# A Fourier layer with a routed expert layer on one core: order of ScalarE's relu, GpSimd's sums and expert pieces in each step

## The chip, the cores and the metric

The kernel runs on one core of a Trainium2 chip. The metric is the device time of one execution in microseconds (us); the runs shown take 745.76, 746.71 and 750.62 us, median 746.71. The engines are called as in the profile: PE is TensorE's matmuls, PEld its weight loads, DVE is VectorE, ACT is ScalarE, POOL is GpSimd, and SP is SyncE, which here only issues DMA transfers.

## The reference, cut to what matters

```python
def _attn_ref(x, w_r, w_i, b_r, b_i):            # x: 8 x 3136 x 256, fp32
    X = np.fft.rfft(x, axis=1)
    Yr = Xr @ w_r - Xi @ w_i + b_r
    Yi = Xr @ w_i + Xi @ w_r + b_i
    Yr = np.sign(Yr) * np.maximum(np.abs(Yr) - lam, 0.0)      # lam = 0.01, Yi alike
    return np.fft.irfft(Yr + 1j * Yi, n=3136, axis=1)

def _moe_ref(x, w_gate, w1, w2, capacity):        # x: what _attn_ref returned; capacity 128
    scores = np.einsum('bsd,d->bs', x, w_gate)
    out = x.copy()
    for b in range(B):
        top_idx = the `capacity` rows of b with the highest scores
        ye = np.maximum(x[b, top_idx] @ w1, 0.0) @ w2
        out[b, top_idx] = x[b, top_idx] + sigmoid(scores[b, top_idx])[:, None] * ye
    return out
```

## The kernel before

Each of the 8 batches goes through a forward transform in two stages, a product with the complex weights, a soft threshold, and an inverse transform in two stages. Between the stages of a transform the data lie in scratch memory in HBM, As on the way forward and Cs on the way back.

- First forward stage: `fold` (lines 420 to 431) makes a sum and a difference of two halves of an input tile xt, two POOL additions at L425 into a tile sd; `s1` (L444) multiplies sd on PE, ACT copies the result to at (L447), and SP stores it to As.
- Second forward stage and the spectrum, in units of one group g of a batch b: `ld_a` loads av from As (four groups at once), and for the last group of two batches together a small tile at, two loads of 64 KB. `s2` (L492, for the last group L500) makes px; ACT casts it to Xh (L504) and DVE takes the rest Xl (L505).
- `spectral` (lines 507 to 526): six matmuls into the second half of the PSUM bank pcb, which ACT copies to ks (L519) and POOL adds to the bias as kb (L521); twelve matmuls into py (L237 to L239 are the lines of the helper that issues all eighteen); DVE adds kb to py (L525).
- `shrink` (lines 528 to 533): ACT's relu r of py (L530) and DVE's Y (L532), which together are the soft threshold.
- First inverse stage, `s2i` (from line 535): eight matmuls from Y (L553) into the first halves of the banks pca and pcb. Then, in this order, ACT copies pca into ct (L565), DVE takes the scores from pcb (L567, a product with the gate's weights that is summed into Csc; the name "junk" is its unused product), ACT copies pcb, and DVE takes the scores from pca. SP stores ct to Cs, where the last stage fetches it as cv.
- Last inverse stage, `s1i` (from line 617), 32 calls in all: 32 matmuls (L626), two ACT copies (L635 into ot, L642 into a tile of the pool sd), and four additions and subtractions on POOL (L639), which `finish` puts into the list adds; the last entry of a call puts the 1 MB store of ot to the output into the list waiting, from where `flush` hands it to SP at the start of a later step. There are two ot buffers, so that a call needs the store of the call before last to be over.
- The expert layer: once a batch's scores are there, `select` finds the 128th score digit by digit with short matmuls into pca (L264) and short DVE instructions (L250 to L286), `place` the rows, `gather` fetches them (xe, L352), and `ffn` multiplies them in pieces: transposes at L363, pairs of matmuls at L388 and single ones at L404. One call of `tick(ffns)` issues one piece.

The order on every engine is written by hand; each engine works its instructions off in that order. The main loop runs over t, one step a unit, with T = 100. A step issues, in this order: the SP stores and loads of the step; s2 of unit t + 1; an s1 if one is due, else one expert piece; the routing's matmuls; spectral of unit t; the fold that is due (L848 to L851; `steady` names the folds that are due); `add(n)`, the next n entries of adds (L852); s1i where the step has one; `ticks` expert pieces (L837); s2i of unit t - 1; shrink of unit t (L869); and finish. After the loop a tail does the routing of the last batch, the rest of s1i and three experts.

## Time and profile before

| | before |
|---|---|
| runs (us) | 745.76, 746.71, 750.62; median 746.71 |
| profiled execution (us) | 751.31 |
| its span, first to last instruction (us) | 749.5 |
| PE busy, share of the span | 666.2 us, 89% |
| PEld | 491.0 us, 66% |
| DVE | 444.6 us, 59% |
| ACT | 377.9 us, 50% |
| POOL | 445.5 us, 59% |
| mean granted clock of PE | 0.96 of 2.4 GHz |

The engines run side by side, so busy times don't add up to the span. A matmul's end is modelled in the profile, and matmuls overlap: a busy PE may still have started its next matmul late, which is seen from the starts alone. The idle time before an instruction and what ended it are in square brackets in a timeline, and in the list of waits as a sum over the program.

### The profile page before, as it was taken

The page shows a single profiled execution, that of the slowest core. Times are in us where ns is not written, and L with a number is a line of the kernel's source. Part 1 is how long each engine was busy: PE and PEld are TensorE (multiplying, and loading weights), DVE is VectorE, ACT ScalarE, POOL GpSimd, SP SyncE. Part 2 cuts the span into 40 slices and gives each one's busy share as a digit, 9 for nine tenths or more (in the row PEclk, how much of TensorE's full clock was granted, in tenths as well). Part 3 has the DMA queues.
Part 4 walks back from the last instruction along what each step waited for, and adds up shares of the span by engine and source line. Part 5 has one row for each costly group of instructions (what it writes and reads, how often), then busy time and mean ns, then how long its engine had stood idle before and what let it go on. Part 6 is the DMA issues. An engine that isn't in the chain of part 4 may idle for free.

```text
span 749.5 us, 21755 instructions
## 1 busy us (share of the span) xinstructions
PE 666.2 (89%) x8923; PEld 491.0 (66%) x8923; DVE 444.6 (59%) x1386; ACT 377.9 (50%) x672; POOL 445.5 (59%) x369
## 2 busy tenths in 40 slices
PE   6599899999898888998999889998998889978896
PEld 2476667766666666776776577665776677656475
DVE  5255556875777465765767455775567566665450
ACT  4155545556556565555555465564555454544310
POOL 1266555367777577666667567675745466475471
PEclk9899999999999899999999899999999999999877
DMA  9979758778788697778587786978484865745650
GB/s 315 324 280 329 240 172 269 242 244 312 224 302 283 241 320 242 257 255 284 162 281 248 254 284 192 329 237 280 147 255 146 271 194 187 232 141 172 211 208 21
DMA packets 96642, 179.62 MB, mean 240 GB/s; under 512 B 5758, under 2 KB 83424, under 8 KB 85216
## 3 DMA queue, kind: packets, MB, share of 16 engines
q1 hardware_dynamic: 95360, 175.96, 69.6%
q0 software_dynamic: 896, 2.17, 0.9%
q8 instruction: 70, 1.15, 0.6%
q14 instruction: 28, 0.23, 0.1%
q10 hardware_dynamic: 288, 0.11, 0.1%
HBM read 92.31 MB, written 85.98 MB: 238 GB/s over the span
## 4 chain that ended last, share of the span: by engine, by line
PE 42%; DVE 14%; POOL 12%; DMA 11%; ACT 10%; issue 9%; SPq 1%; POOLq 0%; DVEq 0%; ACTq 0%
PE pca L553 7%; POOL kb L521 6%; DMA at<-As 4%; PE py L237 4%; DVE junk L567 4%; PE s L444 3%; ACT r L530 3%; PE px L626 3%; POOL sd L425 3%; PE py L238 3%; PE py L239 3%; DVE Xl L505 3%; PE m L388 2%; PE px L492 2%; POOL ot L639 2%
## 5 line engine op out<-in xcount | busy, mean ns | idle before, releaser
L521 POOL TENSOR_TENSOR kb<-ks,bias 128x512 f32<-128x512 f32 x100 | 128.0, 1280 | 228.2 <-ACT ks L519 209.1
L639 POOL TENSOR_TENSOR ot<-ot,sd 128x512 f32<-128x512 f32 x120 | 153.8, 1283 | 4.7
L425 POOL TENSOR_TENSOR sd<-xt 113x512 f32<-113x512 f32 x104 | 130.5, 1279 | 20.0 <-DMA xt<-in_x 20.0
L505 DVE TENSOR_TENSOR Xl<-px,Xh 128x768 fp32r<-128x768 f32 x100 | 95.8, 958 | 44.5 <-ACT Xh L504 44.5
L525 DVE TENSOR_TENSOR py<-py,kb 128x512 f32<-128x512 f32 x100 | 69.8, 698 | 80.1 <-POOL kb L521 62.0
L553 PE MATMUL pca<-Y,gi_sb 64*64 64x256 f32 x760 | 103.2, 390 | 7.6 <-DVE pca L259 4.5
L553 PE MATMUL pcb<-Y,gi_sb 64*64 64x256 f32 x768 | 104.8, 390 | 0.0
L532 DVE SCALAR_TENSOR_TENSOR Y<-py,r 128x512 f32<-128x512 f32 x100 | 69.2, 692 | 45.5 <-ACT r L530 45.4
L565 ACT COPY ct<-pca 128x256 f32<-128x256 f32 x99 | 37.0, 373 | 108.9 <-PE pcb L553 100.3
L492 PEld LDWEIGHTS px<-g_sb,av 64*64 64x64 f32 x3072 | 76.9, 135 | 22.6 <-ACT ot L635 8.0
L504 ACT CAST Xh<-px 128x768 fp32r<-128x768 f32 x100 | 80.9, 809 | 18.1 <-PE px L492 12.8
L492 PE MATMUL px<-g_sb,av 64*64 64x96 f32 x3072 | 83.5, 246 | 5.0 <-DVE Xl L505 2.0
L553 PEld LDWEIGHTS pca<-Y,gi_sb 64*64 64x64 f32 x760 | 46.5, 133 | 56.6 <-DVE pca L259 15.2
L567 DVE CUSTOM_DVE_ANT_0 junk<-pcb,wgb 128x256 f32<-128x256 f32 x100 | 42.3, 423 | 61.0 <-PE pcb L553 54.8
L447 ACT COPY at<-s 128x1024 f32<-128x1024 f32 x58 | 59.6, 1027 | 33.4 <-PE s L444 33.4
L530 ACT ACTIVATE r<-py,m2l 128x512 f32<-128x512 f32 x100 | 69.4, 694 | 5.7 <-DVE py L525 5.7
L237 PE MATMUL py<-wnh,Xh 128*128 128x256 f32 x200 | 63.8, 319 | 7.2 <-DVE Y L532 5.7
L444 PE MATMUL s<-sd,w 64*64 64x512 f32 x480 | 67.8, 623 | 2.4 <-ACT at L447 2.2
L237 PE MATMUL pcb<-wsh,Xh 128*128 128x256 f32 x200 | 66.7, 333 | 3.2 <-ACT ct L565 3.2
L635 ACT COPY ot<-px 128x1024 f32<-128x1024 f32 x30 | 30.4, 1012 | 67.7 <-PE s L626 59.9
L239 PE MATMUL py<-wnl,Xh 128*128 128x256 f32 x200 | 57.3, 286 | 0.0
L238 PE MATMUL py<-wnh,Xl 128*128 128x256 f32 x200 | 57.2, 286 | 0.0
(183 smaller groups left out, 1482.7 us busy)
## 6 DMA issues: line engine op xcount, KB each, us to landing
out<-ot SPq DMA_DIRECT2D x30, 1024.0 KB
xt<-in_x SPq DMA_DIRECT2D x28, 1024.0 KB
av<-As SPq DMA_DIRECT2D x46, 512.0 KB
Cs<-ct SPq DMA_DIRECT2D x23, 1024.0 KB
cv<-Cs SPq DMA_DIRECT2D x90, 256.0 KB
As<-at SPq DMA_DIRECT2D x28, 784.0 KB
cv<-in_x SPq DMA_DIRECT2D x4, 1024.0 KB
out<-at SPq DMA_DIRECT2D x2, 1024.0 KB
```

Of the source, the lines that this page charges most:

```text
L237: nc.tensor.matmul(out, wh, mh, start=start, stop=False)
L238: nc.tensor.matmul(out, wl, mh, start=False, stop=False)
L239: return nc.tensor.matmul(out, wh, ml, start=False, stop=stop).ins
L425: eng.tensor_tensor(out=f[:113, k], in0=t[:113, 0], in1=t[:113, 1], op=op)
L444: nc.tensor.matmul(p[64 * c:64 * c + 64, r, :], w[64 * r:64 + NH * r, v, :], f[64 * r:64 + NH * r], start=(k == 0), stop=(k == len(parts[0 ...
L492: nc.tensor.matmul(o[:, :, N2 * j:N2 * j + N2], a[64 * p:64 * p + 64, j, g % 4, 128 * h + 64 * q:128 * h + 64 * q + 64], g_sb[64 * p:64 * ...
L504: nc.scalar.copy(out=vh, in_=v)
L505: nc.vector.tensor_tensor(out=vl, in0=v, in1=vh.bitcast(F32), op=ALU.subtract)
L521: nc.gpsimd.tensor_tensor(out=kb[:r], in0=ks[:r].broadcast_to([r, 2, D]), in1=bias[:r], op=ALU.add)
L530: nc.scalar.activation(out=r1[:r], in_=py[:r], func=AF.Relu, bias=m2l[:r], scale=1.0)
L553: nc.tensor.matmul(p[q][64 * a:64 * a + 64], gi_sb[64 * q:64 * q + 64, g, c, 64 * a:64 * a + 64], y[64 * q:64 * q + 64, c, :], start=(c == ...
L639: return lambda: nc.gpsimd.tensor_tensor(out=o[:, k, r], in0=o[:, 0, r], in1=q[:, r], op=(ALU.add, ALU.subtract)[k])
```

## The change

There are three edits, all to the order of instructions; none adds or removes arithmetic.

1. The relu of unit t moves on ACT from behind the two copies of s2i(t - 1) to between them. `s2i` takes a function `between`, which it calls after the first copy and the first score; `shrink` takes the finished relu. It holds for steps 1 to T - 2.
2. The four sums of an s1i call: a step that issues a fold (or has one due in the plan, `steady(t + LEAD + 2)`) now takes one entry of adds, another step two; before, a step took two entries of five and then three. The hand-over of the store is no longer an entry of its own but belongs to the last sum.
3. A step issues one or two expert pieces in place of two or three.

```diff
-    def shrink(b, g, py, r):
+    def relu(py, r):
         r1 = pool.tile([128, 2, D], F32, name="r1", bufs=RB)
         nc.scalar.activation(out=r1[:r], in_=py[:r], func=AF.Relu, bias=m2l[:r], scale=1.0)
+        return r1
+
+    def shrink(b, g, py, r, r1=None):
+        r1 = r1 or relu(py, r)
         y = pool.tile([128, 2, D], F32, name="Y", bufs=YB)
         nc.vector.scalar_tensor_tensor(out=y[:r], in0=py[:r], scalar=0.0, in1=r1[:r], op0=ALU.min, op1=ALU.add)
         Y[b, g] = y
 
-    def s2i(b, g):
+    def s2i(b, g, between=None):
...
             nc.vector.tensor_tensor_reduce(out=junk, in0=p[k], in1=wgb, scale=1.0, scalar=0.0,
                                            op0=ALU.mult, op1=ALU.add, accum_out=Csc[bk][:, col:col + 1])
+            if k and between:
+                r1 = between()
...
+        return r1 if between else None
...
         def finish():
             nc.scalar.copy(out=q, in_=p[1])
-            adds.extend([op(0, 1), op(0, 0), op(1, 1), op(1, 0), lambda: waiting.append((done["t"] + 3, store))])
+            last = op(1, 0)
+            adds.extend([op(0, 1), op(0, 0), op(1, 1), lambda: (last(), waiting.append((done["t"] + 3, store)))])
             if b == B - 1:
-                add(5)
+                add(4)
...
-        ticks = 2 + (t % 3 > 0) if t < T - 1 else 0
+        ticks = 1 + (t % 3 > 0) if t < T - 1 else 0
...
-        add(3 if len(adds) < 5 else 2)
+        add(1 if steady(t + LEAD + 2) and len(adds) < 5 else 2)
...
-            s2i(b, g)
+            r1 = s2i(b, g, (lambda: relu(py, r)) if t < T - 1 else None)
...
-            shrink(*units[t], py, r)
+            shrink(*units[t], py, r, r1 if t > 0 else None)
```

ACT, two neighbouring steps in the middle of the loop (ct is the copy of s2i, r with a number is the relu, sd the second copy of s1i). Before:

```order
L565 COPY ct<-pca 128x256
L565 COPY ct<-pcb 128x256
L530 ACTIVATE r_5592<-py,m2l 128x512
L642 COPY sd<-s 128x1024
L504 CAST Xh<-px 128x2x6x64
L519 COPY ks<-pcb 128x256
```

and with the change (its line numbers differ by a few):

```order
L569 COPY ct<-pca 128x256
L530 ACTIVATE r_5577<-py,m2l 128x512
L569 COPY ct<-pcb 128x256
L649 COPY sd<-s 128x1024
L504 CAST Xh<-px 128x2x6x64
L519 COPY ks<-pcb 128x256
```

The relu and the second copy have changed places; what follows them is the same.

POOL, about a period of s1i near step 40 (kb belongs to spectral, sd<-xt is the fold, ot<-ot,sd are the sums). Before:

```order
L521 TENSOR_TENSOR kb<-ks,bias 128x512
L425 TENSOR_TENSOR sd<-xt 113x512 x2
L639 TENSOR_TENSOR ot<-ot,sd 128x512 x2
L521 TENSOR_TENSOR kb<-ks,bias 128x512
L425 TENSOR_TENSOR sd<-xt 113x512 x2
L521 TENSOR_TENSOR kb<-ks,bias 128x512
L639 TENSOR_TENSOR ot<-ot,sd 128x512 x2
L521 TENSOR_TENSOR kb<-ks,bias 128x512
```

and with the change:

```order
L521 TENSOR_TENSOR kb<-ks,bias 128x512
L425 TENSOR_TENSOR sd<-xt 113x512 x2
L646 TENSOR_TENSOR ot<-ot,sd 128x512
L521 TENSOR_TENSOR kb<-ks,bias 128x512
L425 TENSOR_TENSOR sd<-xt 113x512 x2
L646 TENSOR_TENSOR ot<-ot,sd 128x512
L521 TENSOR_TENSOR kb<-ks,bias 128x512
L646 TENSOR_TENSOR ot<-ot,sd 128x512 x2
L521 TENSOR_TENSOR kb<-ks,bias 128x512
```

Between two kb there were up to four POOL instructions, with the change there are at most three, and the four sums of a call end one step later.

SP, the loads of the small tile at for step 60 (at_ with a number) and what stands around them (Cs<-ct stores, out<-ot stores, av and xt loads). Before:

```order
L164 DMA Cs_74<-ct 1024x1x256
L164 DMA out<-ot 128x2048
L164 DMA at_5599<-As 64x1x256 x2
L164 DMA av<-As 128x4x256 x2
L164 DMA As<-at 98x2048
L164 DMA xt<-in_x 128x2048
```

and with the change:

```order
L164 DMA Cs_74<-ct 1024x1x256
L164 DMA at_5586<-As 64x1x256 x2
L164 DMA av<-As 128x4x256 x2
L164 DMA As<-at 98x2048
L164 DMA out<-ot 128x2048
L164 DMA xt<-in_x 128x2048
```

The output store stands a step later, behind the small loads; 19 output stores move in such a way, and at the same place of step 35 it is likewise, while ahead of the loads for step 85 the store stays where it was.

## Rows read from the trace of the kernel before

**Rows 1.** Page, part 1: busy us (share of span) and instructions of PE.

```profile
PE 666.2 (89%) x8923; PEld 491.0 (66%) x8923; DVE 444.6 (59%) x1386; ACT 377.9 (50%) x672; POOL 445.5 (59%) x369
```

**Rows 2.** Waits, whole program: who <- for whom: us in total, times, longest.

```profile
DVE Y L532 <- ACT r L530: 45.4, 99, 0.8
...
ACT ct L565 <- DVE Csc L567: 32.1, 95, 1.3
...
PE py L237 <- DVE Y L532: 5.7, 18, 0.4
...
PE pcb L237 <- ACT ct L565: 3.2, 8, 0.6
```

**Rows 3.** Timeline of PE, step 12: start us, us, engine, instruction; last pcb, first py matmul.

```profile
104.99 0.28 PE L239 MATMUL pcb<-wsl,Xh 128*128 128x256 f32 x1
105.11 0.28 PE L237 MATMUL py<-wnh,Xh 128*128 128x256 f32 x1
```

**Rows 4.** The same two matmuls, steps 2 and 98.

```profile
49.04 0.28 PE L239 MATMUL pcb<-wsl,Xh 128*128 128x256 f32 x1
49.76 0.35 PE L237 MATMUL py<-wnh,Xh 128*128 128x256 f32 x1 [0.44 <-DVE Y L532]
...
675.26 0.28 PE L239 MATMUL pcb<-wsl,Xh 128*128 128x256 f32 x1
675.58 0.36 PE L237 MATMUL py<-wnh,Xh 128*128 128x256 f32 x1
```

**Rows 5.** Timeline of ACT, DVE, PE, step 84 into 85; [idle before <-releaser].

```profile
581.93 0.38 ACT L565 COPY ct<-pca 128x256 f32<-128x256 f32 x1 [2.57 <-PE pcb L553]
582.09 0.42 DVE L567 CUSTOM_DVE_ANT_0 junk<-pcb,wgb 128x256 f32<-128x256 f32 x1 [0.19 <-PE pcb L553]
...
582.56 0.37 ACT L565 COPY ct<-pcb 128x256 f32<-128x256 f32 x1 [0.25 <-DVE Csc L567]
...
582.83 0.69 ACT L530 ACTIVATE r<-py,m2l 128x512 f32<-128x512 f32 x1
...
583.55 0.69 DVE L532 SCALAR_TENSOR_TENSOR Y<-py,r 128x512 f32<-128x512 f32 x1 [0.45 <-ACT r L530]
...
584.07 0.28 PE L239 MATMUL pcb<-wsl,Xh 128*128 128x256 f32 x1
...
584.39 0.35 PE L237 MATMUL py<-wnh,Xh 128*128 128x256 f32 x1
```

**Rows 6.** Waits of ACT's relu, and POOL's groups by line (busy us, mean ns, idle before).

```profile
ACT r L530 <- DVE py L525: 5.7, 2, 3.4
...
L639 POOL TENSOR_TENSOR ot<-ot,sd 128x512 f32<-128x512 f32 x120 | 153.8, 1283 | 4.7
```

**Rows 7.** Timeline of SP and PE around the small loads for step 60.

```profile
404.48 0.61 SPq L164 DMA_DIRECT2D out<-ot  x1
405.15 2.28 SPq L164 DMA_DIRECT2D at<-As  x2
...
413.59 0.38 PE L553 MATMUL pcb<-Y,gi_sb 64*64 64x256 f32 x2
414.37 0.54 PE L500 MATMUL px<-gt_sb,at 64*64 64x192 f32 x4 [0.40 <-DMA at<-As]
416.27 1.22 PE L500 MATMUL px<-gt_sb,at 64*64 64x192 f32 x10 [1.36 <-DMA at<-As]
```

**Rows 8.** Stretches: PE, PEld, DVE, ACT, POOL busy (x), PEclk, DMA share, GB/s.

```profile
200.00:300.00 100.00, 89.92 (x1296) 65.41 (x1293) 62.52 (x195) 55.72 (x99) 68.53 (x55) 0.97 0.82 275
```

**Rows 9.** Chain that ended last: start us, us, two runs of expert matmuls.

```profile
310.86 0.89 PE m L388 x8
...
317.98 1.06 PE m L404 x4
```

**Rows 10.** Timelines of SP and ACT: an output store, and the reuse of its buffer.

```profile
493.89 1.10 SPq L164 DMA_DIRECT2D out<-ot  x1
...
509.82 1.01 ACT L635 COPY ot<-px 128x1024 f32<-128x1024 f32 x1 [3.17 <-PE s L626]
```

## The prediction

> **What bounds the kernel now.** The page comes first: PE is busy for 89% of the span [rows 1], all others for 50 to 66%, so a gain has to come out of PE's path. The list of waits comes second. PE's own entries are small: it is put down as waiting 5.7 us for Y and 3.2 us for the copies [rows 2]. But the profile models a matmul's end, and a matmul that starts late behind a modelled end leaves no idle time. So I read PE's starts in the timeline, third. Each step has six matmuls into pcb and then twelve into py. Where nothing holds them, the first py matmul starts 0.12 us after the last pcb matmul [rows 3]. In step 2 it starts 0.72 us after, in step 98 0.32 us after [rows 4], in step 85 0.32 us after, which is 0.15 us after Y ended at 584.24 [rows 5]. Py may not be overwritten before Y has read it, so Y holds PE. From step 2 to 98 I count 69 of 97 starts held like this (step 2 is the first, step 98 the last), together 17.2 us over the free spacing.
>
> Why is Y late? Y waits 45.4 us for the relu, in 99 steps [rows 2]. The relu stands behind both copies on ACT, and the second copy waits for DVE's score from the same bank: 32.1 us in 95 steps, 0.34 us each [rows 2]. In one of them [rows 5] the first copy ends at 582.31, the pcb score at 582.51, the second copy runs from 582.56 to 582.93, the relu from 582.83 to 583.52, and Y starts at 583.55 after DVE stood idle for 0.45 us.
>
> **Edit 1, the relu between the copies.** ACT starts a second instruction 0.10 us before the first one ends (582.83 against 582.93 [rows 5]). Put right behind the first copy, the relu runs from 582.21 to 582.90. DVE is free from 583.55 - 0.45 = 583.10, so Y starts at 583.13 in place of 583.55: 0.42 us earlier, more than the 0.20 us by which py was held in this step (0.32 less 0.12). The second copy then starts at 582.80 in place of 582.56, 0.24 us later; the score of pcb is long over. Behind that copy PE's next pcb matmul is queued, and behind that all of PE. In nine steps, nearly the eight that the list has as waits for the copy [rows 2], that matmul starts 0.05 us after it, so nine times 0.24 = 2.2 us are lost; elsewhere PE is busy with px and s1 or with the routing first. SP's Cs store waits for the copy too, 0.24 us, which a transfer of several us hides. ACT's last of the three ends at 583.17 in place of 583.52, so the cast Xh, Xl and DVE's selection chain behind it come 0.35 us earlier. The relu now needs kb's addition to py earlier, and would hold the second copy if that were late; it has waited for it only twice, 5.7 us [rows 6].
>
> The Trainium skill (PSUM — Partial Sum Buffer, section "PSUM bank collisions raise a hardware error") says that two engines may not touch one bank on the same partitions at once, reads included, while different banks are free. The trace agrees for the copy, which starts 0.05 us after the score ends [rows 5]; by that rule the relu, which reads py's bank, need not wait for it. If ACT had to wait for any DVE read of PSUM, the relu would start at 582.56, Y would gain 0.27 in place of 0.42 us, and the sum would end some 8 us higher.
>
> Bounds of edit 1: where PE binds every step, 17.2 - 2.2 = 15 us; where ACT's and DVE's chain binds every step, the idle time that the relu fills, 32.1 us. Both kinds of step stand in the trace, so I take the middle, 24 us.
>
> **Edit 2, the sums.** One sum takes 1.28 us [rows 6]; all 120 remain. A step with a fold had kb, two fold instructions and two sums, five times 1.28 = 6.4 us, against a mean step of (675.26 - 49.04) / 96 = 6.5 us [rows 4]: POOL came late to the next kb as soon as a step was shorter. With one sum the step has 5.1 us. What that gave to the path is bounded by the relu's waits for py, 5.7 us [rows 6], and by nothing, since most late kb are covered by PE's own work. I take 2 us.
>
> What moves with the sums is the store. The last sum of a call falls a step later, so 19 of the 1 MB output stores are issued a step later and change places on SP's queue. Twice (steps 35 and 60) a store leaves the place right ahead of the small loads at, for which PE waits. In step 60 [rows 7] the store is issued at 404.48, the loads at 405.15, PE is through with s2i at about 413.97 (413.59 + 0.38), waits 0.40 us and then 1.36 us for the loads and goes on at 416.27. 1 MB at the 275 GB/s of a full stretch [rows 8] is 3.8 us. Without it ahead, the last load lands at about 412.5, before PE asks. That is 1.76 us at each of two places, 3.5 us; a third such place, in step 85, keeps its store ahead. Ends: 0 us if the loads' lateness has another cause, 7 us if the slow restart behind the wait goes too. I take 4 us.
>
> The Trainium skill (DMA: Bandwidth & Descriptors, section "Queues, rings and completion order") says that a DMA engine takes a ring's descriptors in order. By that the store's transfer time comes off the landing, 4 us in the sum; if a small load could overtake, it would be 0. The trace leans to the rule: 128 KB took 11.1 us from issue to the last matmul's release [rows 7].
>
> **Edit 3, the expert pieces.** They are moved, not removed. Eight L388 matmuls, four pieces, take 0.89 us [rows 9], so a step loses about 0.22 us of pieces where an expert runs and gains it where none ran. Four matmuls of the fifth expert slide behind the loop into the tail, at most 1.06 us [rows 9], where filler matmuls stood. Thinner pieces may fill PE's waits for the routing. I take 0, with ends of -1 and +2 us.
>
> **Sum.** 24 + 2 + 4 + 0 = 30 us. The profiled execution took 751.3 us, 4.6 us over the median of the runs; 751.3 - 30 = 721.3, and on the scale of the runs 717 us. The low ends give 15 + 0 + 0 - 1 = 14 us, 733; the high ends 32 + 6 + 7 + 2 = 47 us, 700. The forecast's own range is 700 to 733.
>
> **Rivals.**
> - The transfers become the bound. The DMA share is already 0.82 between 200 and 300 us [rows 8]; steps that are 4% shorter ask for 0.86, and av, xt or cv may come late. Then half of edit 1 is lost, 12 us: 717 + 12 = 729 us. For it: PE waited for at [rows 7]. Against: the other loads are issued two or more steps ahead, and at is the only one with a wait of weight.
> - PE is really busy, and the late starts are how the profile draws pipelined matmuls. Then only the listed waits go, 5.7 us for Y less 2.2 us for the copy, about 743 us, no change that shows. For it: 89% busy [rows 1]. Against: the same two matmuls lie 0.12 us apart when Y is early [rows 3] and 0.72 us when it is late [rows 4].
> - Slower: the output store, a step later, is not over when its buffer is wanted. For the tightest of them: issue at 493.89, ACT writes the buffer again at 509.82, 15.9 us [rows 10]. A step less leaves 9.4 us. A store that needed as long as at did, 11.1 us [rows 7], would hold ACT's ot copy, all of ACT behind it and PE's px for 1.7 us. It decides against the kernel once the mean hold over 19 stores passes (30 + 7.5) / 19 = 2.0 us; at 3 us each the time is 717 + 57 = 774 us. Against: the store stands ahead of at in the queue and so ends sooner than 11.1 us, and the other stores have more room.
> - The change doesn't do what it says: excluded by the order of the instructions.
>
> **Chances.** A measurement of this kernel tells about 1% from no change, so faster is under 739.2 us and slower over 754.2 us. The forecast has 0.72, a still larger gain (under 700 us) 0.03, the transfers 0.10: faster 0.85. The busy PE has 0.09, all of it within 1%. The late stores have 0.06, slower. The range of 700 to 738 us takes in the forecast and the transfers' case, 0.82.
>
> **What would show it.** Right: the wait of the second copy for DVE's score falls from 32.1 us to nearly 0, Y's wait for the relu falls from 45.4 us to below 10, py starts 0.12 us after pcb in nearly all steps, and PE's waits for at shrink to the place in step 85. Wrong: PE's waits for the second copy rise well over 3.2 us (edit 1 gives its gain back at pcb); ACT's ot copy waits for a DMA (late stores); the relu's wait for py grows over 6 us (kb late, with the copy and PE held behind it); PE waits for av or cv (transfers); or the tail is longer by more than 1 us.

## The result, and the profile after

The changed kernel takes 719.69 us, the median of three runs (714.92 to 721.53), where the kernel before takes 746.71: a ratio of 0.9612, with a 95% interval of 0.9522 to 0.9703. Timed again beside its own variants it took 715.35 us against 746.47 (ratio 0.957, 0.9525 to 0.9616). The forecast was 717 us. The profiled execution of after took 714.92 us, its span is 713.2 us.

The page, part 1 (busy us, share of the span, instructions), to be read beside [rows 1]:

```profile
PE 641.6 (90%) x8920; PEld 481.4 (68%) x8920; DVE 444.5 (62%) x1386; ACT 371.1 (52%) x672; POOL 445.6 (62%) x369
```

PE's work is the same, and it is put down as busy for 24.6 us less. Part of that is the clock: the profiled execution of before ran at a mean of 0.960 and that of after at 0.974, which is 11.4 us less time lost to the lower level (749.5 * 0.040 less 713.2 * 0.026) at most, if PE was busy whenever the clock was low. The rest fits matmuls that the profile drew as running while they were held.

The waits of the whole program (who waits <- for whom: us in total, times, longest), to be read beside [rows 2, 6]. Lines have moved: Y is L536, the copies ct L569, ot L642.

```profile
ACT ot L642 <- DMA out<-ot: 14.3, 4, 4.0
...
ACT r L530 <- DVE py L525: 6.6, 7, 2.2
...
PE pcb L237 <- ACT ct L569: 5.4, 7, 1.3
...
PE px L492 <- ACT ot L642: 4.8, 4, 2.1
...
PE px L500 <- DMA at<-As: 3.0, 3, 1.4
...
DVE Y L536 <- ACT r L530: 2.4, 7, 0.8
```

Y's wait for the relu has gone from 45.4 to 2.4 us. The second copy's wait for the score (32.1 us before) is no longer in the list. The first line is new.

The timeline of step 84 into 85 in after (start us, us, engine, instruction), the place of [rows 5]:

```profile
554.87 2.63 POOL L646 TENSOR_TENSOR ot<-ot,sd 128x512 f32<-128x512 f32 x2
...
556.13 0.37 ACT L569 COPY ct<-pca 128x256 f32<-128x256 f32 x1 [2.57 <-PE pcb L557]
556.28 0.43 DVE L571 CUSTOM_DVE_ANT_0 junk<-pcb,wgb 128x256 f32<-128x256 f32 x1 [0.20 <-PE pcb L557]
556.40 0.69 ACT L530 ACTIVATE r<-py,m2l 128x512 f32<-128x512 f32 x1
...
556.98 0.37 ACT L569 COPY ct<-pcb 128x256 f32<-128x256 f32 x1
...
557.21 0.69 DVE L536 SCALAR_TENSOR_TENSOR Y<-py,r 128x512 f32<-128x512 f32 x1
...
558.26 0.28 PE L239 MATMUL pcb<-wsl,Xh 128*128 128x256 f32 x1
558.38 0.28 PE L237 MATMUL py<-wnh,Xh 128*128 128x256 f32 x1
```

Y starts 1.08 us after the first copy (557.21 - 556.13), where it started 1.62 us after it before. ACT goes through copy, relu, copy without a gap. The first py matmul follows the last pcb matmul by 0.12 us. By the starts in the timeline this is so in 94 of the 97 steps, where it was in 28 before.

The new wait, at its longest, in the timeline of step 36 of after (two windows):

```profile
233.74 0.35 SPq L164 DMA_DIRECT2D out<-ot  x1
...
243.06 0.39 PE L557 MATMUL pcb<-Y,gi_sb 64*64 64x256 f32 x2
...
244.44 1.01 ACT L642 COPY ot<-px 128x1024 f32<-128x1024 f32 x1 [4.03 <-DMA out<-ot]
245.35 0.38 ACT L569 COPY ct<-pca 128x256 f32<-128x256 f32 x1
245.51 1.27 PE L492 MATMUL px<-g_sb,av 64*64 64x96 f32 x32 [2.06 <-ACT ot L642]
```

An output store issued at 233.74 releases its buffer 10.7 us later. ACT stands for 4.03 us, both ct copies and the relu stand behind it, and PE waits 2.06 us for px. This is the slower rival's mechanism, at four places and not at all 19.

### The profile page after: what moved, and what is told of

It is laid out like the page before. It is cut to its first block, busy times and chain, and to the rows that moved or that the text cites. A ratio compares the mean times of both kernels' runs of the same rounds, so it can differ in the third digit from the quotient of the medians.

```text
span 713.2 us, 21863 instructions
## 1 busy us (share of the span) xinstructions
PE 641.6 (90%) x8920; PEld 481.4 (68%) x8920; DVE 444.5 (62%) x1386; ACT 371.1 (52%) x672; POOL 445.6 (62%) x369
## 4 chain that ended last, share of the span: by engine, by line
PE 44%; POOL 15%; DMA 13%; ACT 10%; DVE 9%; issue 7%; SPq 1%; POOLq 0%; ACTq 0%; DVEq 0%
PE pca L557 8%; DMA out<-ot 5%; POOL kb L521 4%; POOL sd L425 4%; POOL ot L646 4%; PE s L444 4%; PE py L237 3%; PE py L238 3%; PE py L239 3%; PE pcb L237 3%; PE px L492 3%; DMA at<-As 3%; PE px L633 2%; ACT r L530 2%; ACT Xh L504 2%
## 5 line engine op out<-in xcount | busy, mean ns | idle before, releaser
L425 POOL TENSOR_TENSOR sd<-xt 113x512 f32<-113x512 f32 x104 | 130.4, 1277 | 19.4 <-DMA xt<-in_x 19.4
L504 ACT CAST Xh<-px 128x768 fp32r<-128x768 f32 x100 | 82.3, 823 | 16.5 <-PE px L492 12.6
L569 ACT COPY ct<-pca 128x256 f32<-128x256 f32 x99 | 37.0, 374 | 97.7 <-PE pcb L557 87.5
L571 DVE CUSTOM_DVE_ANT_0 junk<-pcb,wgb 128x256 f32<-128x256 f32 x100 | 42.4, 424 | 65.2 <-PE pcb L557 61.1
L536 DVE SCALAR_TENSOR_TENSOR Y<-py,r 128x512 f32<-128x512 f32 x100 | 68.6, 686 | 2.4 <-ACT r L530 2.4
L444 PE MATMUL s<-sd,w 64*64 64x512 f32 x480 | 65.5, 608 | 1.5 <-ACT at L447 1.2
L642 ACT COPY ot<-px 128x1024 f32<-128x1024 f32 x30 | 30.4, 1013 | 65.2 <-PE s L633 43.2
L237 PE MATMUL py<-wnh,Xh 128*128 128x256 f32 x200 | 56.8, 284 | 0.2 <-DVE Y L536 0.2
L239 PE MATMUL pcb<-wsl,Xh 128*128 128x256 f32 x200 | 56.7, 284 | 0.0
L238 PE MATMUL pcb<-wsh,Xl 128*128 128x256 f32 x200 | 56.7, 283 | 0.0
```

What stands on the lines that cost most here:

```text
L237: nc.tensor.matmul(out, wh, mh, start=start, stop=False)
L238: nc.tensor.matmul(out, wl, mh, start=False, stop=False)
L239: return nc.tensor.matmul(out, wh, ml, start=False, stop=stop).ins
L425: eng.tensor_tensor(out=f[:113, k], in0=t[:113, 0], in1=t[:113, 1], op=op)
L444: nc.tensor.matmul(p[64 * c:64 * c + 64, r, :], w[64 * r:64 + NH * r, v, :], f[64 * r:64 + NH * r], start=(k == 0), stop=(k == len(parts[0 ...
L504: nc.scalar.copy(out=vh, in_=v)
```

## The experiments

Twelve kernels were run, each five rounds beside the kernel before on the same chip. They fall into four sets on four chips: the kernels with one edit and store_mix; sums_pieces, relu_sums, after_again and store_behind; pieces_thick, relu_fill and behind_fill; behind_start alone. So across sets the ratios are to be compared, and a difference of 2 us in the last column says nothing, since before itself lies between 719 and 721 there. The table holds all of them. "Clock" is the mean over the runs of the mean granted TensorE clock (1 is 2.4 GHz throughout, 0.5 would be 1.2 GHz throughout). "Span x clock" is the mean of span times clock: the span less half the time at the lower level, an estimate of what the kernel would take if the clock never fell and PE set the pace wherever it had fallen.

| kernel | us | ratio to before (95%) | clock | span x clock |
|---|---|---|---|---|
| before (four times) | 746.5 to 747.6 | 1 | 0.964 to 0.968 | 719 to 721 |
| relu_only | 733.49 | 0.9843 (0.9812 to 0.9874) | 0.959 | 702.4 |
| sums_only | 740.96 | 0.9906 (0.9878 to 0.9934) | 0.969 | 715.6 |
| pieces_only | 739.28 | 0.9883 (0.9858 to 0.9907) | 0.975 | 719.0 |
| sums_pieces | 735.25 | 0.9833 (0.9796 to 0.9871) | 0.976 | 715.3 |
| relu_sums | 720.79 | 0.9646 (0.9610 to 0.9681) | 0.968 | 696.6 |
| after_again | 715.35 | 0.957 (0.9525 to 0.9616) | 0.977 | 698.1 |
| pieces_thick | 722.93 | 0.9679 (0.9649 to 0.9708) | 0.972 | 700.6 |
| relu_fill | 734.28 | 0.9835 (0.9801 to 0.9868) | 0.970 | 710.6 |
| store_mix | 712.58 | 0.9549 (0.9518 to 0.9581) | 0.973 | 692.7 |
| store_behind | 708.25 | 0.9472 (0.9439 to 0.9505) | 0.976 | 689.9 |
| behind_fill | 718.65 | 0.960 (0.9565 to 0.9635) | 0.973 | 696.7 |
| behind_start | 705.13 | 0.9454 (0.9413 to 0.9495) | 0.980 | 690.7 |

### One edit at a time

**relu_only**, the kernel before with this part of the change alone:

```diff
+            if k and between:
+                r1 = between()
-            s2i(b, g)
+            r1 = s2i(b, g, (lambda: relu(py, r)) if t < T - 1 else None)
```

> The kernel before with edit 1 alone: the relu stands between the two copies, the sums and the expert pieces are as before. Theory (PE was held by a late Y in 69 of 97 steps and ACT and DVE idled 32 us for each other): 24 us less than the kernel before, 747 - 24 = about 723 us (bounds 15 to 32 us less); Y's wait for the relu falls from 45.4 us to under 5, the second copy's wait for the score from 32.1 us to nearly 0, py starts 0.12 us after pcb in over 85 of 97 steps, and ACT never waits for an output store, since the stores stand where they stood. PE's waits for the small loads at stay near 6.4 us. Rival (PE is really busy, the gain of the whole change came from the sums and the moved store): about 743 us.

Measured: 11.7 us less (747.23 * 0.0157; interval 9.4 to 14.0), not 24. The signs in the trace came as expected: Y's wait for the relu is 2.1 us, and py follows pcb by 0.12 us in 95 of 97 steps. PE's waits for the small loads did not stay near 6.4 us, they are 8.6. Step by step against the trace of before, 55 steps are shorter, by 18.4 us together, 29 are the same within 0.15 us, 7 are longer by 2.3 us together, and 6 differ by over 0.8 us. So the rival (PE busy) falls, and the size of the term does too. The 62 steps that moved by 0.15 to 0.8 us say some 16 us, all 97 together 20.3 us (the two profiled executions, 751.31 and 730.94 us, lie as far apart), the runs 12, and the clock of the runs is the lowest of all, 0.959.

One of the signs of wrong that the prediction named stands in this trace too: the relu waits for DVE's addition to py, and that for kb on POOL. In before these two waits were 5.7 and 62.0 us:

```profile
DVE py L525 <- POOL kb L521: 80.5, 67, 3.2
...
ACT r L530 <- DVE py L525: 15.0, 18, 2.4
```

**sums_only**:

```diff
-        add(3 if len(adds) < 5 else 2)
+        add(1 if steady(t + LEAD + 2) and len(adds) < 5 else 2)
```

(with the last sum and the store's hand-over in one entry, as in the change)

> The kernel before with edit 2 alone: one sum in a step with a fold, two in others, and the output store queued a step later. Theory of the forecast: 6 us less, about 741 us (bounds 0 to 13 less), with the small loads at no longer late in steps 35 and 60 (PE's wait for them from 6.4 us to 3 or less). Rival from the trace of the changed kernel: the later stores hold ACT's ot copy there (14.3 us in 4 places) and give that gain back; steps are longer here than in the changed kernel, so these holds should be shorter, under 8 us: 744 to 749 us, no change that shows.

Measured: 7.0 us less (4.9 to 9.1), as forecast. Waits of sums_only:

```profile
ACT ot L635 <- DMA out<-ot: 11.3, 4, 3.9
...
PE px L500 <- DMA at<-As: 2.7, 3, 1.5
```

PE's wait for at fell from 6.4 us in the list of before to 2.7, and steps 35 and 60 went from 9.06 and 9.35 us to 5.26 and 6.78. The late stores are there too, longer than the rival had it (11.3 us, not under 8), and still the gain stands. A part of the gain comes from a place that was not in the sum: step 75 takes 6.64 us in place of 10.64. In before the fourth expert begins there, and PE waits 2.21 us for its gathered rows xe; in sums_only the expert begins in step 76, and the wait is gone.

**pieces_only**:

```diff
-        ticks = 2 + (t % 3 > 0) if t < T - 1 else 0
+        ticks = 1 + (t % 3 > 0) if t < T - 1 else 0
```

> The kernel before with edit 3 alone: one or two expert pieces a step in place of two or three. Theory: 746 us, from 1 us more to 2 us less; PE's waits for Csc in the routing, 18.0 us before, a little less or the same. Rival (thinner pieces leave PE alone in steps where it waits for the routing, or the experts slide into the tail): 3 us or more over the kernel before.

Measured: 8.7 us less (7.0 to 10.6). Neither theory held: the term was not nothing, and the sign was the good one. The steps of the two traces show where it comes from. The lengths of some steps in us, before and pieces_only:

```
step     45    46    47    48    73    83
before  5.86  7.28  7.01  5.77  5.12  6.22
pieces  5.40  6.87  6.59  5.33  5.76  6.86
```

Steps 45 to 48 belong to an expert in both, and each is 0.41 to 0.46 us shorter. Steps 46 to 48 hold one piece less now. Step 45 holds two pieces in both (eight records of L388), and shows why the place matters. In before both run at once, and PE then waits for Csc; in pieces_only one of them runs where PE had waited (timelines of PE, before and then pieces_only):

```profile
310.70 1.05 PE L388 MATMUL m<-xT,w1s 128*128 128x128 f32 x8
...
314.03 0.39 PE L264 MATMUL pca<-digits,n 128*128 128x15 f32 x2 [0.59 <-DVE Csc L567]
```

```profile
309.62 0.61 PE L388 MATMUL m<-xT,w1s 128*128 128x128 f32 x4
...
311.84 0.71 PE L388 MATMUL m<-xT,w1s 128*128 128x128 f32 x4
312.50 0.39 PE L264 MATMUL pca<-digits,n 128*128 128x15 f32 x2
```

In the list of waits this one goes from 18.0 us (27 times) to 10.8 us (18 times). Steps 73 and 83 had no piece and now have six and four records of L404; they are 0.64 us longer. Step 75 is shorter here too, 6.30 us in place of 10.64, again because the fourth expert begins in step 76.

### The edits in company

The three gains alone add up to 27.4 us, the whole change measured 27 to 32. The next three kernels look whether that is more than chance.

> The changed kernel itself, timed beside its own variants. Each edit alone gave, as a ratio to the kernel before: relu 0.9843 (747.23 * 0.0157 = 11.7 us less), sums 0.9906 (7.0 less), pieces 0.9883 (8.7 less); together 27.4 us, so 720 us if the edits simply add, which is what the changed kernel took before (719.69). Mean granted clock as before, 0.972.

**sums_pieces** is the change without its first edit:

```diff
-            r1 = s2i(b, g, (lambda: relu(py, r)) if t < T - 1 else None)
+            s2i(b, g)
```

> The changed kernel with edit 1 undone (the relu behind both copies again), edits 2 and 3 kept. If the edits simply add: 747.2 - 7.0 - 8.7 = 731.5 us, so edit 1 is worth 11.7 us here too. Rival, from the granted clocks of the runs (relu alone ran at a mean of 0.959, before at 0.968, pieces alone at 0.975): edit 1 by itself is worth the 18 us that its steps show in the trace (55 steps shorter by 0.33 us each), and alone gave some 6 us of it back because PE ran more of the time at the lower clock. With the other edits the clock stays up, so here edit 1 is worth 17 to 19 us: 719.7 + 18 = about 738 us, at a clock of 0.972 or more.

Measured: 735.25 against 715.35 us, so edit 1 is worth 19.9 us here, where alone it was worth 11.7. The edits don't simply add. Nor do edits 2 and 3: beside each other they are worth 12.5 us (746.47 * 0.0167), and 15.7 alone. Step 75 accounts for a difference of this size: each of them alone takes some 4 us out of it, and both together (6.30 us) no more. The waits of sums_pieces show edit 1's two waits back:

```profile
DVE Y L532 <- ACT r L530: 45.1, 98, 0.8
...
ACT ct L565 <- DVE Csc L567: 26.1, 95, 1.3
```

From its trace to that of after_again 57 steps are shorter, by 19.4 us together, 29 are the same, 6 are longer by 2.4 us together, and 5 differ by over 0.8 us (1.4 us longer together).

**relu_sums** is the change without its third edit:

```diff
-        ticks = 1 + (t % 3 > 0) if t < T - 1 else 0
+        ticks = 2 + (t % 3 > 0) if t < T - 1 else 0
```

> The changed kernel with edit 3 undone (two or three expert pieces a step again), edits 1 and 2 kept. If the edits simply add: 747.2 - 11.7 - 7.0 = 728.5 us. Rival by the clock (edit 3 shortens the steps by about 2 us only and gives the rest by keeping PE at the higher clock): the mean granted clock falls to about 0.963 from 0.972, which is 2 * 0.009 * 718 = 13 us more at half the clock and 6 us more in all, with 2 us of steps: about 727 to 728 us; the two differ in the clock that the runs show (0.970 or over if the clock has no part in it).

Measured: 720.79 us, 5.4 us over after_again, and 7 us under what either theory had. The clock is 0.968 against 0.977, as the rival said, and span x clock is no higher (696.6 and 698.1). Since edit 1 alone, edit 2 brought 14.7 us in the ratios (0.9843 to 0.9646): it is edits 1 and 2 that need each other, by some 7 us. A part of that stands in the traces: with edit 2 the relu's wait for py goes from 15.0 us to

```profile
ACT r L530 <- DVE py L525: 10.2, 11, 2.7
```

In six of the steps in which the relu waited in relu_only (0.19 to 0.98 us) neither edit alone gives much, both together 2.6 us; the wait is gone from all six, and the clock is 1.00 in all of them, in each of the four traces (lengths in us):

```
step        27    30    32    33    41    71   sum
before     6.77  6.22  5.51  6.17  6.62  6.30  37.6
relu_only  6.69  6.15  5.37  6.32  6.65  6.22  37.4
sums_only  6.77  6.22  5.51  6.03  6.39  6.22  37.1
relu_sums  6.32  5.94  5.17  5.93  5.71  5.94  35.0
```

So about 2 us of the 7 are POOL's: with edit 1 the relu asks for py earlier, kb is late for it, and edit 2 brings kb earlier (DVE's wait for it is 61.6 us in relu_sums, 80.5 in relu_only). In the column of span x clock nothing is left of the 7 us: edit 1 is worth 18.7 alone (721.1 - 702.4), 19.0 beside edit 2 (715.6 - 696.6) and 17.2 beside both; edit 2 5.5 alone and 5.8 beside edit 1; edit 3 2.1 alone and -1.5 beside both. Some of these differences are taken across sets, with the 2 us of doubt said above.

**pieces_thick** goes the other way with edit 3:

```diff
-        ticks = 1 + (t % 3 > 0) if t < T - 1 else 0
+        ticks = 3 + (t % 3 > 0) if t < T - 1 else 0
```

> The changed kernel with three or four expert pieces a step in place of one or two; all else kept. With two or three it took 720.8 us at a mean clock of 0.968, with one or two 715.4 at 0.977. Theory by the clock (thicker pieces leave more steps in which PE has no expert work and waits for the routing, and the clock falls behind these waits): clock 0.966 or less, time 721 to 726 us, while span times mean clock stays at 696 to 699 us. Rival (thick pieces cost by the steps' own length): span times clock grows by 3 us or more; second rival: no change from 720.8 at two or three, since the waits are where the routing is, whatever the pieces.

Measured: 722.93 us: 715.4, 720.8, 722.9 us with one or two, two or three, three or four pieces. But its clock is 0.972, not 0.966 or less, so the theory by the clock isn't borne out. What takes its place is open: pieces_thick ran on another chip than the other two, by ratio it lies within the interval of relu_sums (0.9679 and 0.9646), so that the second rival, no change, stands, and span x clock is 700.6, too near to 696.6 and 698.1 to tell a cost of the steps' own length.

### What a fall of the clock costs

The profile of relu_only, stretches of step 75 and of step 85 (us, then busy us of PE, PEld, DVE, ACT, POOL with instructions, granted clock, DMA share, GB/s), with PE's timeline of step 75 ahead:

```profile
498.28 0.28 PE L239 MATMUL py<-wdl,Xh 128*128 128x256 f32 x1
501.51 0.68 PE L363 MATMUL m<-ident,xe 128*128 128x128 f32 x2 [2.95 <-DMA xe<-out,idx]
```

```profile
498.00:501.00 3.00, 0.56 (x5) 0.36 (x4) 2.18 (x9) 0.00 (x0) 2.91 (x3) 1.00 0.99 371
501.00:504.50 3.50, 2.99 (x18) 1.27 (x22) 0.76 (x3) 0.53 (x2) 0.85 (x1) 0.58 0.45 153
...
570.00:573.00 3.00, 1.57 (x18) 0.89 (x18) 0.66 (x3) 0.21 (x2) 1.81 (x2) 1.00 1.12 332
573.00:576.50 3.50, 3.50 (x19) 3.50 (x18) 1.12 (x2) 1.06 (x2) 1.27 (x1) 0.53 0.81 326
```

PE waits for the gathered rows for 2.95 us at a clock of 1.00, and the next stretch, full of work, runs at 0.58. In step 85 it waits twice for the small loads at, 1.2 and 1.4 us, and the next stretch runs at 0.53. The Trainium skill (TensorE: Matmul & The Clock Gate, section "HAM oscillation — how this bites in real kernels") says that a PE that waits for a transfer can find its clock halved when the data come, and starts its next work slowly; these rows agree. Not every such wait is followed by a fall, though: in after PE waits 0.74 and 1.44 us for the same loads in step 85, and step 86 runs at a clock of 1.00.

**relu_fill** is relu_only with filler matmuls, whose results nothing uses, ahead of such waits:

```diff
         if g == G - 1:
+            idle(4)
             for h in range(2):
                 for k in range(2):
+                    idle(4 if h == 0 and k else 0)
...
+            idle(8 if item[0] == B - 1 else {3: 10}.get(e, 0))
...
+        idle({50: 8, 63: 6, 75: 6, 88: 5, 96: 6}.get(t, 0))
         turn("pe", "da")
```

> The kernel with edit 1 alone, with filler matmuls ahead of PE's longest waits: 4 ahead of each half of the small at tiles' matmuls (four times), 10 ahead of the fourth expert's transposes (a wait of 3.0 us), 5 to 8 ahead of five waits for Csc in the routing (1.3 to 2.2 us each). Theory (edit 1 is worth 18 us, of which the kernel with it alone gave 6 back by a mean clock of 0.959 against 0.964 to 0.968 before): the clock rises to about 0.968 and the time falls by 4 to 8 us, to 726 to 730 us, with nothing of the work removed. Rival (edit 1 alone is worth only 12 us): 733 us or more, since the fillers are added work.

Measured: 734.28 us, the same as relu_only, at a clock of 0.970, as the theory had it. The time did not follow, since two of the fillers made waits of their own: they write the bank s and were queued behind ACT's sd copy in steps 49 and 74, which grew from 7.91 and 7.39 to 12.12 and 11.15 us. Where the fillers ran inside the wait, the step tells what a fall had cost. The same stretch of relu_fill, 572 to 580 us, behind the waits of step 85:

```profile
572.00:580.00 8.00, 7.59 (x79) 5.16 (x92) 3.79 (x12) 2.39 (x5) 5.22 (x5) 1.00 1.09 348
```

The clock stays at 1.00. The lengths of the steps, relu_only and relu_fill (steps 63, 86 and 96 come right after a wait, step 75 holds one):

```
step        62    63    75    85    86    96
relu_only  6.97  7.07 11.09  7.46  7.39  7.50
relu_fill  7.41  5.52  8.60  7.54  5.84  5.96
```

Steps 86 and 96 are 1.55 and 1.54 us shorter with nothing of their work removed. That is the price of one fall that the fillers kept away; by its sum in time, though, the experiment says nothing on whether the falls make up the 6 us that edit 1 lost alone.

### The late stores

**store_mix** hands the store over a step earlier, but keeps it behind the small loads at:

```diff
-  waiting.append((done["t"] + 3, store))
+  waiting.append((done["t"] + 2 + (units[min(done["t"] + 5, T - 1)][1] == G - 1), store))
```

> The changed kernel with each output store queued one step earlier (as soon as the step with its last sum is over), except where that step loads the small at tiles first; there it stays behind them. In the trace of the changed kernel ACT waits 14.3 us, in 4 places, for a store that still reads the buffer, and POOL's last sum is over 4.5 to 10.6 us before its store is queued. Theory (these holds are on the path: in one of them PE stands 0.6 us before px is free, in another 1.0 us, and all of ACT starts 4 us late): the waits go, 2 to 8 us less than the changed kernel, 712 to 718 us where that one takes 719.7. Rival (the holds lie beside PE's routing and expert work, or SP now waits for POOL's last sum with other loads queued behind it): as the changed kernel, 719 to 722 us, with SP's loads av and cv later.

**store_behind** keeps them only behind the at loads of their own step:

```diff
-  waiting.append((done["t"] + 3, store))
+  waiting.append((done["t"] + 2, store))
...
-        flush()
+        late = t + 3 < T and units[t + 3][1] == G - 1
+        flush(not late)
...
+        if late:
+            flush()
         for b, i in loads[t] if t >= 0 else ():
```

> The changed kernel with each output store queued as soon as the step with its last sum is over, and in the steps that load the small at tiles right behind those loads in the same step, not a step later. In the trace of the version with the store a step earlier, two of the four waits of ACT's ot copy for a store were left (8.1 us, at the two steps whose store was kept back behind at). Theory: both go, ACT's wait for out<-ot under 2 us, PE's waits for at as there (under 2.5 us); 2 to 4 us less than that version's 712.6, 709 to 711 us. Rival (the two waits lay beside other waits of PE): 712 to 713 us.

Measured: 712.58 us for store_mix, within its theory, and 708.25 for store_behind, a little below its theory and 7.1 us under after_again in the same set. The wait of ACT's ot copy for a store is 8.1 us in two places in store_mix,

```profile
ACT ot L642 <- DMA out<-ot: 8.1, 2, 4.0
```

and gone from the list of store_behind, where PE's own waits for at stay small:

```profile
PE px L500 <- DMA at<-As: 1.1, 2, 0.8
```

Not all of the 7.1 us is ACT's waits. From after_again to store_behind the steps with a late store and the ones behind them (36, 37, 39, 61 and 64) are 5.5 us shorter together. Step 85 is 2.8 us shorter for another reason: its store no longer stands ahead of the small loads, and PE's two waits for them, 0.84 and 1.46 us, are gone. So some 14 us of ACT's waits cost about 5.5 us. The slower rival had the mechanism; in after it amounts to 0.75 us a store (14.3 / 19), under the 2.0 us from which it would decide.

### One long step

**behind_fill** was to show the price of the clock in store_behind:

```diff
+            idle(8 if item[0] == B - 1 else {3: 7}.get(e, 0))
...
+        idle({53: 16, 89: 7}.get(t, 0))
         turn("pe", "da")
```

> The version with the store behind at, with filler matmuls (their results are not used) where its trace shows PE waiting: 16 ahead of the wait of 4.2 us for Csc in step 52, 7 ahead of the one of 1.8 us in step 88, 7 ahead of the fourth expert's transposes, where PE waits 1.9 us. Nothing of the work is removed. In that version the granted clock is at its lower level for 3.4 us after each of the three. Theory (a long wait costs its length and then again by the lower clock): these three stretches go, the mean clock of the runs rises from 0.976 to about 0.985, and up to 1.7 us each is saved, 3 to 5 us in all: 703 to 706 us where that version takes 708.3. Rival (the lower clock costs nothing, or doesn't come from the waits): 708 us or, by the fillers' own time, up to 710.

Measured: 718.65 us, some 10 us slower. As in relu_fill, the fillers of steps 52 and 88 stood behind ACT's copy out of the bank s and ran after the wait (timeline of behind_fill):

```profile
348.08 1.03 ACT L649 COPY sd<-s 128x1024 f32<-128x1024 f32 x1
...
349.17 4.05 PE L676 MATMUL s<-wsh 128*128 128x512 f32 x10 [5.33 <-ACT sd L649]
```

Only those ahead of the fourth expert's transposes ran in time: step 76 went from 9.97 to 8.38 us. That the fillers did it is not shown, since without any of them this step takes 8.41 us in after, 8.43 in after_again and 8.37 in store_mix, with the clock up; the fall in store_behind may be a matter of the single execution. The wait of step 52 in store_behind has a cause that I had not looked for (timeline of DVE, POOL and PE):

```profile
340.06 2.48 POOL L425 TENSOR_TENSOR sd<-xt 113x512 f32<-113x512 f32 x2
...
341.08 2.97 DVE L369 CUSTOM_DVE_ANT_0 junk<-xe,wgb 128x256 f32<-128x256 f32 x1
342.51 1.25 POOL L646 TENSOR_TENSOR ot<-ot,sd 128x512 f32<-128x512 f32 x1
...
345.29 0.16 PE L319 MATMUL pca<-cnt,tm 98*98 98x2 bf16 x1 [4.18 <-DVE Csc L571]
```

The expert's gate score takes 2.97 us beside POOL's instructions, the scores Csc stand behind it on DVE, and PE waits 4.18 us.

**behind_start** moves that expert by one piece, and keeps the fillers that ran in time:

```diff
+            if e == 1:
+                yield
+            idle(8 if item[0] == B - 1 else 7 if e == 3 else 0)
```

> The version with the store behind at, with two small edits: the second expert starts one piece later, so that its transposes, their copy and its gate score on DVE (L369) stand behind Csc, Y and Xl of step 52 and not ahead of them; and 7 filler matmuls ahead of the fourth expert's transposes. In that version L369 took 2.97 us in step 52, where POOL ran two fold instructions and a sum without a gap, and 0.54 us in steps 42 and 88; ACT, DVE's Csc and PE stood behind it, and the granted clock fell after it; steps 52 and 53 took 10.4 and 7.9 us. Theory: both steps come to 6 to 6.7 us, 5 us less together, and step 76 to 8.4 us in place of 10.0, which the fillers already gave in the version that had them; together 6 to 7 us, 701 to 703 us where that version takes 708.3. Rival (the long L369 moves with the expert, or the wait in step 52 has another cause, the routing that runs there): 706 to 708 us, with L369 over 1.5 us or a wait over 2 us still in step 52 or 53.

Measured: 705.13 us, 3 us less than store_behind by the medians and 1.3 by the ratios, less than half of what was expected. Step 52 fell from 10.41 to 6.92 us, and step 53 rose from 7.94 to 10.75: L369 takes 0.41 us now, but the copy xT ahead of it stands behind Xl on DVE, and the expert's own matmuls wait for it (timeline of behind_start):

```profile
346.05 0.41 DVE L369 CUSTOM_DVE_ANT_0 junk<-xe,wgb 128x256 f32<-128x256 f32 x1
346.19 0.71 PE L388 MATMUL m<-xT,w1s 128*128 128x128 f32 x4 [2.06 <-DVE xT L366]
```

The wait went with the expert, as the rival had it for the wait; the time lies between theory and rival. Step 76 was 1.6 us shorter (8.38 us, as in the kernels without fillers), and the fall of the clock behind step 88 was absent in this profile (step 89 6.91 in place of 8.48 us), though nothing had been done there. This is the fastest version by its median; its interval and that of store_behind overlap, so it cannot be told from that one.

## Why the prediction came out right

The time was right to 3 us, and the sum was right only in total: 30 us forecast, 29.0 measured (746.71 * 0.0388; interval 22.2 to 35.7). The mechanism of edit 1, the largest term, was right. That the total came out so near is luck: two of its terms were off, in opposite directions, and the terms measured alone don't add up to the whole in the way the sum took for granted.

- **Edit 1, mechanism right, size too high.** Y follows the first copy by 1.08 us where the working said 1.20 (583.13 - 581.93), and the second copy by 0.85 where it said 0.87. The relu starts at 556.40 while DVE reads pcb, so a read of another bank does not hold it, and the costlier reading of the rule, that any read of PSUM by DVE would, is out. The waits for the relu and the score fell as listed. The step that failed is "so I take the middle": between 15 and 32 us I took 24, and the runs gave 11.7 us alone and 19.9 beside the other two. In relu_only 29 of the 97 steps stayed the same within 0.15 us, and a few got longer. Some of them had no late Y to begin with (steps 51, 55, 79, 80 and 90 hold expert pieces, and the distance of py from pcb is the same 0.12 us in both traces); others gave it back at the second copy, for which PE waits 6.4 us in relu_only and 5.4 in after in place of 3.2 (0.96 us in step 8, one of the 29), and others at the relu itself, which had to wait for py (steps 27, 30, 32, 41 and 71 are among the 29). The low end, 15 us, had been worked out from the steps where Y held PE, and lay nearer; alone the edit gave less than that, too.
- **Edit 2, right.** 6 us forecast, 7.0 measured alone. Inside it errors cancel: the small loads gave more than 3.5 us (steps 35 and 60 went from 9.06 and 9.35 to 5.26 and 6.78 us in sums_only, 6.4 us), step 75 gave 4.0 us that were not in the sum, and the late stores took some of it back (11.3 us of ACT's waits there). The third place, step 85, kept its store and its wait, as said: in after PE waits there up to 1.4 us. The bound for POOL, the relu's waits for py, was read from a trace in which the relu stood late. With edit 1 alone they are 15.0 us, with edits 1 and 2 10.2, in after 6.6. So the 2 us taken for POOL are there, about that much in the six steps shown, but only beside edit 1. Not every kb became early: four fold instructions still stand ahead of that of step 8, more than the three named with the change, and there the relu waits 1.4 us in after.
- **Edit 3, wrong.** 0 with ends of -1 and +2 us was forecast; 8.7 us were measured alone and 5.4 beside the others. Some 4 us of the 8.7 are step 75, which edit 2 gives as well, so that beside it they don't count again. Two steps of the argument failed. "Eight L388 matmuls, four pieces" misread the profile, which has two records for each of these matmuls: all eight experts have 256 records of L388, 32 each, where the loop over F = 1024 issues 16. A piece is thus about 0.45 us, and not 0.22; a step with one piece less is 0.41 to 0.44 us shorter (46 to 48). And "gains it where none ran" took each moved piece to cost its full time in the new place. From relu_sums to after_again 26 steps get shorter by 12.6 us together, and only 11 get longer, by 4.9 us; 11 more differ by over 0.8 us and are 1.4 us longer together. A part of the pieces went into steps in which PE stood waiting for the routing, as in step 45. In the list PE's wait pca <- Csc went from 18.0 us before to 10.8 in pieces_only, and from 14.7 in relu_sums to 8.4 in after_again. Against this stands the new long wait of step 52, which is 2.9 us longer in after_again than in relu_sums.
- **The rivals.** Transfers did not become the bound: PE waits 0.8 us for av and 0.3 us for xt in the whole of after. PE was not really busy: the relu alone made the kernel 11.7 us faster, where this rival left room for 3.5 us (5.7 less 2.2). (At 4% shorter steps the DMA share would have been 0.85 and not 0.86, which changes nothing.) The slower rival came in part: 14.3 us of ACT's waits, worth some 5.5 us by store_behind, which the forecast's sum did not hold. The tail, from the start of step 99 on, is 65.9 us in after and 68.5 in after_again, where it was 67.9, so no growth is shown.
- **Not settled:** how much of the rest of the interaction between edits 1 and 2 (7 us, of which about 2 are POOL's), and of edit 3, is the clock. Span x clock makes edit 1 worth 17 to 19 us in any company and edit 3 worth about nothing, which would put all of it on the clock. But pieces_thick did not have the clock that this would give, and relu_fill raised the clock without lowering the time, since its fillers cost as much as they saved. And whether a fall follows a wait differs between profiles, so a single trace doesn't tell the price of an edit to a few us.

## What to carry to other kernels

When two engines wait for each other in every step, give the waiting one the independent instruction that stands behind; price the gain from the steps where the late result really holds the bound engine, and take the rest for nothing until shown. Ask what the moved instruction now has to wait for: an input that was always in time may be late for it, and bringing that input earlier is then worth something only beside the move. When a filler's or a transfer's place changes, look at once for the buffer that it holds: a store issued a step later, or a filler in a bank that another engine still reads, becomes a new wait. Work in small pieces is cheapest in the steps where the bound engine waits anyway, so spread it thin, and count pieces from the code, not from records.

## What was not expected of the hardware

- **A DVE instruction with both inputs in SBUF (L369) stretches beside POOL's TENSOR_TENSOR.** Alone it took 0.41 us. Started beside a POOL instruction it mostly took the rest of that one and 0.28 us more (0.54 to 1.48 us); in step 52 of after and of store_behind it was over only behind the third of three that followed each other without a gap, after 2.96 and 2.97 us. L571, the same operation with one input in PSUM, took 0.43 us beside a running sum (556.28 in the timeline of after). Nothing else on DVE that often ran beside POOL was slowed in the traces of before and after: L250, which reads one tensor from SBUF, took 0.62 us alone and beside POOL. The Trainium skill (GPSIMD Engine Reference, section "2. Architecture") says that POOL's physical read port is shared with DVE; the rows agree, and they show that the DVE instruction can wait for more than one POOL instruction.
- **A wait can be paid for again behind it.** Ahead of the two falls shown PE had waited 2.95 us in the one place, 1.2 and 1.4 us in the other; where fillers kept the clock up, the step behind was about 1.55 us shorter. It is not certain: behind waits much like these (0.74 and 1.44 us in after, step 85; the fourth expert's, step 76) one profile has a fall and another has none.
- **An output store of 1 MB held its buffer for 10.7 us** from its issue, where 275 GB/s [rows 8] would have moved it in 3.8 us.
